# Splitting the output products of a decode attention kernel into two column groups with their own PSUM banks, casts and stores

## Chip, core and metric

The kernel runs on one core of one Trainium2 chip. Times are device microseconds (us) of whole executions. The granted clock is the share of the full TensorE clock that the profile shows. A packet is one piece of a load, moved by one of the core's 16 DMA engines.

## The reference

It is one decode step: attention over a cache of 4,096 positions for 2 rows and 32 heads, mixed by a gate with a small MLP.

```python
g = sigmoid((x * gate_w).sum(-1, keepdims=True))
q = (x @ wq)                                   # 2 rows, 32 heads of 128
p = softmax(q . k_cache * 128 ** -0.5)         # k_cache, v_cache: 2 x 32 x 4096 x 128, bf16
a = (p . v_cache) @ wo                         # wo: 4096 x 512
b = relu(x @ w1) @ w2
out = g * a + (1 - g) * b                      # 2 x 512
```

The keys and values are 134 MB of the 145.46 MB that must be read.

## The kernel before

There are eight stages `s`, each of 8 heads of one row: 8.4 MB of keys and 8.4 MB of values. In a stage VectorE multiplies four parts of the keys by the query (`mult`). Three of the four parts are then summed in groups by TensorE through products with the identity (`red`), and finished by a short VectorE sum (`scores`). The second part is summed by VectorE alone, in 8.7 us.

```python
    for s in range(NS):
        ...                                  # work of stages s-1 and s-2 woven in
        mult(s, 2)
        scores(s, 1)                         # VectorE's own long sum
        red(s, 2)
        mult(s, 3)
        scores(s, 2)
        red(s, 3)
        if s == NS - 1:
            pv(s - 1)
        scores(s, 3)                         # waits for red(s, 3) on TensorE
        probs(s)
        ...
        if s + 2 < NS:
            load_k(s + 2)                    # two key buffers: waits until stage s is read
            load_v(s + 1)                    # one value buffer: waits for pv(s)
        if s == NS - 2:
            load_v(NS - 1)
            load_wo()                        # into the value buffer: waits for pv(NS - 2)
```

The tail accumulates 11 MLP products (issued early) and 32 attention products, each 512 columns wide with 2 rows of output, into one PSUM tile, then casts and stores it:

```python
    a_ps = apool.tile([B, D], fp32, name="a_ps")
    def accumulate(lhsT, rhs, start, stop):
        nc.tensor.matmul(a_ps, lhsT=lhsT, rhs=rhs, start=start, stop=stop)
    ...
    evac(s)
    wo_mm(0)                                 # 8 products with the first 1 MB of wo
    comb(s)                                  # the last selector product: lhsT is a selection matrix
    unpack(s)
    for g in range(1, NG):
        wo_mm(g)
    nc.vector.tensor_copy(out=res[:, : D // 2], in_=a_ps[:, : D // 2])
    nc.scalar.copy(out=res[:, D // 2 :], in_=a_ps[:, D // 2 :])
    nc.sync.dma_start(out=out[:, 0, :], in_=res)
```

wo comes in six loads: three of 1 MB, and the last 1 MB cut in pieces of 512, 256 and 256 KB.

The softmax here doesn't subtract the row's maximum and nothing guards it: scores larger than these inputs give would overflow.

## Time and profile before

| | us |
|---|---|
| median of 6 runs before the prediction | 347.06 (346.87 to 349.65) |
| span of the profiled run | 345.3 |
| wo loads issued from | 326.83 |
| last 16 output products | 338.81 to 342.42 |
| casts, store issued | 342.46, 342.90, 343.29 |

These lines are from the page of the kernel before: the DMA busy share in tenths in 40 equal slices of the span; the DMA queues with packets, MB and the share of the 16 engines' time; and the shares of the chain that ended last (the page's walk back from the last instruction, at each step to what released it).

```profile
DMA  7999999898999989899999999999999999989993
...
q1 hardware_dynamic: 4036, 145.46, 97.9%
q8 instruction: 8, 0.13, 0.2%
...
DVE 65%; PE 16%; DMA 12%; issue 5%; SPq 0%; ACT 0%; DVEq 0%
```

The chain names VectorE for 65%.

The timeline of the tail (start, duration, engine, line, operation, operands; in brackets the idle time before it and what ended it):

```profile
326.83 3.85 SPq L369 DMA_DIRECT2D vt<-in_A_wo_dram  x6
...
338.81 3.61 PE L354 MATMUL a_ps<-vt,OT_sb 128*2 128x512 bf16 x16 [0.61 <-DMA vt<-in_A_wo_dram]
...
342.46 0.41 DVE L439 CAST res<-a_ps 2x256 bf16<-2x256 f32 x1 [5.62 <-PE a_ps L354]
342.90 0.36 ACT L440 CAST res<-a_ps 2x256 bf16<-2x256 f32 x1 [18.35 <-DVE res L439]
343.29 0.33 SPq L441 DMA_DIRECT2D out_dram<-res  x1
```

The products run at 226 ns each, and ScalarE's cast starts only after VectorE's.

The waits of VectorE, with the total, how often, and the longest:

```profile
DVE sc L231 <- PE red L219: 38.4, 9, 5.2
DVE kt L210 <- DMA kt<-in_A_k_cache_dram: 22.7, 1, 22.7
```

38.4 us are spent waiting for the identity matmuls (`red`). The 22.7 us are the start, when the first keys have not landed.

### The profile page before, as it was taken

Reading aid. Unit: us, or ns where it says so; the run is one execution under the profiler, and the core shown is the slowest. Engines: PE = TensorE matmul, PEld = TensorE weight load, DVE = VectorE, ACT = ScalarE, POOL = GpSimd, SP = SyncE. Lnnn points to the kernel's source line nnn. Section 1 sums busy time; section 2 is a strip of 40 time slices with the busy share of each in tenths; the row PEclk is TensorE's granted clock in tenths of the full one; section 3 lists DMA queues with packets and bytes.
Section 4 is the critical chain, followed back from the end, with each engine's and each line's share of the span. In section 5 each row is a group of like instructions: output and inputs, shape, how many; then the busy total and the mean of one; then the engine's idle time right before and its main releaser. Section 6 shows DMA issues by size and latency. Waiting matters only on the chain.

```text
span 345.3 us, 2525 instructions
## 1 busy us (share of the span) xinstructions
PE 182.3 (53%) x1107; PEld 76.0 (22%) x1107; DVE 254.1 (74%) x151; ACT 7.5 (2%) x23; POOL 6.1 (2%) x16
## 2 busy tenths in 40 slices
PE   0420685158506843655644761566165464477965
PEld 0100232023202311222211320223022221132432
DVE  3002269949994999499967999499939996799530
ACT  1010000000000000000000000000000000000000
POOL 7000000000000000000000000000000000000000
PEclk9995566788978888689868887889768896688999
DMA  7999999898999989899999999999999999989993
GB/s 308 474 433 392 464 440 478 372 486 364 480 395 455 478 375 471 387 463 397 448 478 395 463 397 448 410 440 473 402 455 410 440 419 425 478 387 418 416 410 141
DMA packets 4051, 145.60 MB, mean 422 GB/s; under 512 B 453, under 2 KB 586, under 8 KB 970
## 3 DMA queue, kind: packets, MB, share of 16 engines
q1 hardware_dynamic: 4036, 145.46, 97.9%
q8 instruction: 8, 0.13, 0.2%
q14 instruction: 1, 0.01, 0.0%
q10 hardware_dynamic: 6, 0.00, 0.0%
HBM read 145.46 MB, written 0.00 MB: 421 GB/s over the span
## 4 chain that ended last, share of the span: by engine, by line
DVE 65%; PE 16%; DMA 12%; issue 5%; SPq 0%; ACT 0%; DVEq 0%
DVE kt L210 37%; DVE sc L231 20%; PE red L219 14%; DMA kt<-in_A_k_cache_dram 9%; DVE PT_sb L251 4%; DMA vt<-in_A_wo_dram 3%; DVE osb L289 2%; PE a_ps L354 1%; PE o_ps L276 1%; DVE OT_sb L316 1%; DVE tmp L307 0%; DVE osb L287 0%; DVE rsg L268 0%; SPq L369 0%; DVE rsg L267 0%
## 5 line engine op out<-in xcount | busy, mean ns | idle before, releaser
L219 PE MATMUL red<-kt,ident 128*128 128x512 bf16 x400 | 125.5, 484 | 123.1 <-DVE kt L210 123.1
L210 DVE TENSOR_TENSOR kt<-kt,qb 128x8192 bf16<-128x8192 bf16 x32 | 141.3, 4417 | 31.5 <-DMA kt<-in_A_k_cache_dram 22.7
L219 PEld LDWEIGHTS <-ident 128*128 128x128 bf16 x400 | 47.9, 120 | 199.1 <-issue 163.5
L231 DVE TENSOR_REDUCE sc<-kt 128x64 f32<-128x8192 bf16 x7 | 60.8, 8679 | 0.0
L231 DVE TENSOR_REDUCE sc<-red 128x64 f32<-128x512 f32 x25 | 17.2, 687 | 38.4 <-PE red L219 38.4
L276 PE MATMUL o_ps<-vt,PT_sb 128*32 128x512 bf16 x448 | 27.1, 398 | 10.2 <-DMA vt<-in_A_v_cache_dram 10.2
L276 PEld LDWEIGHTS <-PT_sb 128*32 128x32 bf16 x512 | 14.7, 100 | 25.1 <-issue 13.9
L251 DVE TENSOR_TENSOR PT_sb<-e,tmask 128x2048 bf16<-128x2048 bf16 x8 | 18.3, 2283 | 0.6 <-ACT e L237 0.6
L237 ACT ACTIVATE e<-sc 128x256 bf16<-128x256 f32 x8 | 3.3, 417 | 274.7 <-DVE sc L231 274.7
L289 DVE SCALAR_TENSOR_TENSOR osb<-o_ps,jmask,osb 128x128 f32<-128x128 f32 x24 | 8.4, 351 | 0.8
L354 PE MATMUL a_ps<-vt,OT_sb 128*2 128x512 bf16 x32 | 7.4, 378 | 2.2 <-DMA vt<-in_A_wo_dram 2.2
L257 PE MATMUL gs<-partials,heads 128*128 128x1 f32 x16 | 3.0, 259 | 9.7 <-ACT e L237 9.7
L195 PE MATMUL mm<-vt 128*32 128x512 bf16 x64 | 5.5, 505 | 4.9 <-DMA vt<-in_A_wq_dram 4.2
L307 DVE SCALAR_TENSOR_TENSOR tmp<-comb,rsg,umask 128x128 f32<-128x128 f32 x8 | 2.8, 347 | 4.1 <-PE comb L301 4.1
L257 PEld LDWEIGHTS gs<-partials,heads 128*128 128x128 f32 x16 | 2.4, 188 | 13.6 <-ACT e L237 11.3
L354 PE MATMUL a_ps<-vt,hT 128*2 128x512 bf16 x11 | 4.9, 630 | 0.5 <-ACT hT L347 0.5
L159 PE MATMUL comb<-ident,vt 2*128 2x2 bf16 (+1 forms) x8 | 0.6, 173 | 7.6 <-DMA vt<-in_gate_w_dram 5.4
L439 DVE CAST res<-a_ps 2x256 bf16<-2x256 f32 x1 | 0.4, 413 | 5.6 <-PE a_ps L354 5.6
L276 PE MATMUL o_ps<-kt,PT_sb 128*32 128x512 bf16 x64 | 3.8, 380 | 1.1 <-DMA kt<-in_A_v_cache_dram 1.1
L354 PEld LDWEIGHTS <-OT_sb 128*2 128x2 bf16 x32 | 2.7, 83 | 6.6 <-issue 2.8
L195 PEld LDWEIGHTS <-vt 128*32 128x32 bf16 x64 | 2.2, 119 | 7.8 <-issue 7.2
L287 DVE TENSOR_SCALAR osb<-o_ps,jmask 128x128 f32<-128x128 f32 x8 | 2.8, 347 | 1.2 <-PE o_ps L276 1.2
(40 smaller groups left out, 33.9 us busy)
## 6 DMA issues: line engine op xcount, KB each, us to landing
vt<-in_A_wq_dram SPq DMA_DIRECT2D x1, 4096.0 KB, 12.4
kt<-in_A_v_cache_dram SPq DMA_DIRECT2D x1, 4096.0 KB, 25.9
kt<-in_A_v_cache_dram SPq DMA_DIRECT2D x2, 2048.0 KB, 34.8
vt<-in_A_wo_dram SPq DMA_DIRECT2D x3, 1024.0 KB, 9.1
vt<-in_B_w_dram SPq DMA_DIRECT2D x1, 1376.0 KB, 34.2
vt<-in_B_w_dram SPq DMA_DIRECT2D x1, 1280.0 KB, 36.8
vt<-in_A_wo_dram SPq DMA_DIRECT2D x1, 512.0 KB, 10.9
vt<-in_A_wo_dram SPq DMA_DIRECT2D x2, 256.0 KB, 11.0
```

The source lines that it names most:

```text
L195: nc.tensor.matmul(ps[j * CG : (j + 1) * CG, :], lhsT=xbp[:, b, c, e, :], rhs=wq_v[:, c, 2 * j + e, :, :], start=(c == 0 and e == 0), stop ...
L210: nc.vector.tensor_tensor(out=kt, in0=kt, in1=q, op=ALU.mult)
L219: nc.tensor.matmul(ps, lhsT=ident, rhs=prod[:, :, j * RW : (j + 1) * RW], start=(j == 0), stop=(j == Dh // RW - 1),)
L231: nc.vector.reduce_sum(out=sc_t[s][:, u * CU : (u + 1) * CU], in_=red_t.pop((s, u)), axis=AX.X)
L237: nc.scalar.activation(out=e, in_=sc_t.pop(s), func=ACT.Exp, scale=inv_sqrt_dh, accum_out=partials[:, s : s + 1],)
L251: nc.vector.tensor_tensor(out=out_, in0=e.to_broadcast(shape), in1=m.to_broadcast(shape), op=ALU.mult)
L257: nc.tensor.matmul(rs_t[s], lhsT=heads.rearrange("p t a -> p (t a)"), rhs=partials[:, s : s + 1], start=True, stop=True,)
L276: nc.tensor.matmul(o_t[s][k * CG : (k + 1) * CG, :], lhsT=PT_sb[:, s % 2, q, :], rhs=v_t[s][:, q * JB : (q + 1) * JB, :], start=(q < NCG), ...
L287: nc.vector.tensor_scalar_mul(osb, o[:, 0, :], jmask[:, 0:1])
L289: nc.vector.scalar_tensor_tensor(out=osb, in0=o[:, j, :], scalar=jmask[:, j : j + 1], in1=osb, op0=ALU.mult, op1=ALU.add,)
L316: nc.vector.reduce_sum(out=OT_sb[:, g, :, b], in_=tmp, axis=AX.X)
L354: nc.tensor.matmul(a_ps, lhsT=lhsT, rhs=rhs, start=start, stop=stop)
```

## The change

The intent is to let the products of two halves of the columns run side by side in two column groups of the TensorE array, to give each half its own bank so that the two casts need not take turns, and to store each half as soon as it is cast. The bank of the small sums is given up for it. The last selector product goes ahead of all output products.

```diff
-    a_ps = apool.tile([B, D], fp32, name="a_ps")
+    halves = []
+    for e in range(2):
+        a_ps = apool.tile([P, D // 2], fp32, name=f"a_ps{e}")
+        halves.append((e * CG, a_ps[e * CG : e * CG + B], slice(e * (D // 2), (e + 1) * (D // 2))))
 ...
-        rs_t[s] = gsp.tile([P, 1], fp32, name="gs")
+        rs_t[s] = mmp.tile([P, NG * Dh], fp32, name="mm")[:, :1]
 ...
-        nc.tensor.matmul(a_ps, lhsT=lhsT, rhs=rhs, start=start, stop=stop)
+        for _, a, cols in halves:
+            nc.tensor.matmul(a, lhsT=lhsT, rhs=rhs[:, cols], start=start, stop=stop)
 ...
-    wo_mm(0)
     comb(s)
     unpack(s)
-    for g in range(1, NG):
+    for g in range(NG):
         wo_mm(g)
-    res = ...  # two casts in turn, one store
+    copies = (nc.vector.tensor_copy, nc.scalar.copy)
+    for (p, a, cols), copy, queue in zip(halves, copies, (nc.sync, nc.scalar)):
+        res = consts.tile([P, D // 2], bf16, name=f"res{p}")[p : p + B]
+        copy(out=res, in_=a)
+        queue.dma_start(out=out[:, 0, cols], in_=res)
```

Each of 43 products becomes two, and each product is two instructions (weights, matmul). The program therefore has 86 more TensorE rows.

More of the change, by code (lines that the diff above doesn't have):

```diff
@@ L71 @@
     combp = ctx.enter_context(tc.tile_pool(name="combp", bufs=1, space=PS))
-    gsp = ctx.enter_context(tc.tile_pool(name="gsp", bufs=1, space=PS))
     apool = ctx.enter_context(tc.tile_pool(name="apool", bufs=1, space=PS))
@@ L431 @@
     evac(s)
-    wo_mm(0)
     comb(s)
     unpack(s)
-    for g in range(1, NG):
+    for g in range(NG):
         wo_mm(g)
-    res = consts.tile([B, D], bf16, name="res")
-    nc.vector.tensor_copy(out=res[:, : D // 2], in_=a_ps[:, : D // 2])
-    nc.scalar.copy(out=res[:, D // 2 :], in_=a_ps[:, D // 2 :])
-    nc.sync.dma_start(out=out[:, 0, :], in_=res)
+    copies = (nc.vector.tensor_copy, nc.scalar.copy)
[3 more added lines that the diff above has]
+        queue.dma_start(out=out[:, 0, cols], in_=res)
 _INS = ['A_x', 'A_k_cache', 'A_v_cache', 'A_wq', 'A_wo', 'B_x', 'B_w1', 'B_w2', 'gate_w']
```

## The prediction

> **What bounds the kernel now.** The span is 345.3 us. In the chain of work that ended last, VectorE has 65%, TensorE 16%, DMA 12%: from 32.7 us to 323 us it is VectorE's products and sums (L210, L231) and the identity matmuls they wait for (5.0 to 5.8 us of wait in stages 1 to 6). None of that is touched. The change works on the last 22 us, and on 11 matmuls at 45.9 us.
>
> In order of time, the tail of the chain reads: the wo loads until 338.76; 16 output products from 338.81 to 342.42 (3.61 us, 226 ns each at granted clock 1.00); VectorE cast 342.46, 0.41 us; ScalarE cast 342.90, 0.36 us, which waited for VectorE's; store issued 343.29; then about 2 us for its landing and the program's end.
>
> **What the change does.**
> 1. Each 512-column product becomes two of 256 columns in different column groups and banks. The trace already shows column groups overlapping: the last 64 o_ps matmuls (512 columns, four groups) take 3.64 us, 57 ns each, against 226 ns for a lone a_ps product. Two groups should give about 113 ns for a pair, so 16 products need about 1.8 us instead of 3.6. The Trainium skill ("TensorE: Matmul & The Clock Gate", Part 3) says the same of column tiles.
> 2. But the weights bind then. In the windows by stage, DMA share is still 0.65 from 339.0 to 340.0 and reaches zero only near 340.8; products of the last rows wait for their own pieces. I expect the last piece at about 340.9, two pairs after it (0.23 us) and the pipeline's end: casts start near 341.35 instead of 342.46. So about 1.1 us of the 1.8 us is kept.
> 3. The casts run side by side. Now one waits for the other; the Trainium skill ("PSUM — Partial Sum Buffer", bank collisions) says that two engines may not read one bank in the same quadrant at once, which is why they were ordered. Separate banks take 0.4 us off. Both stores land side by side; I allow 0.1 us for the second.
> 4. The last selector product ahead of the output products: it frees nothing that counts. Now it runs at 335.64, OT_sb is ready at 336.8, and the product that needs it waits for weights until 338.8. Worth 0.
> 5. The 11 MLP products at 45.9 us take 4.86 us at clock 0.50; perhaps 2.4 us after. TensorE is then idle until 55.26 anyway, and the V load behind them issues 2 us earlier onto a busy DMA queue. Worth 0.
> 6. Sharing the mm bank with the small sums: no other user is alive by then. Worth 0.
>
> **Prediction.** Sum: 1.1 + 0.4 = 1.5 us off 347.06: 345.6 us, 0.4% faster; range 344.9 to 346.7. Chances: faster by over 2% 0.01, within 2% 0.98, slower by over 2% 0.01.
>
> **What would show it.** Right: in the timeline the output products come in bursts of about 0.9 us for 8 pairs, with waits for wo before the last ones; both casts start within 0.1 us; the store issues near 341.7; VectorE's chain before 323 us keeps its times. Wrong: pairs at 226 ns (no overlap), no wait for the last wo pieces, casts still in turn, or the ScalarE store landing last by far.
>
> **What would make it wrong.** A later DMA tail (the slowest engine's last packets), a lower TensorE clock from the gaps between bursts, or a shift of the clock's phase in the stages, which moves 5 us waits by some tenths.

## More of the kernel before

The queue line says that the 16 DMA engines were at work for 97.9% of the span, and the slice line reads 8 or 9 tenths everywhere but in the first and the last slice. Note also the line `q8 instruction`: the program's own instructions come by DMA too, 8 packets, 0.13 MB, so 16 KB each.

## The result

The changed kernel took 347.9 us in the median of 10 runs (347.10 to 349.11). The kernel before took 347.45 in the median of 20 runs (346.76 to 349.90). The ratio of the means is 0.9999, with an interval of 0.9975 to 1.0023. The predicted 1.5 us did not come, and the time lies outside the predicted range.

The same parts of the page of the changed kernel:

```profile
DMA  8999999898999989999999999999999999999994
...
q1 hardware_dynamic: 4036, 145.46, 98.0%
q8 instruction: 9, 0.15, 0.2%
...
DVE 65%; PE 16%; DMA 12%; issue 5%; SPq 1%; DVEq 0%
```

These lines look nearly alike. The one difference that turns out to count: `q8 instruction` has 9 packets now, not 8. The timeline of the changed kernel's tail:

```profile
328.31 3.31 SPq L372 DMA_DIRECT2D vt<-in_A_wo_dram  x6
...
338.49 0.27 PE L357 MATMUL a_ps_140<-vt,OT_sb 128*2 128x256 bf16 x1 [1.45 <-DMA vt<-in_A_wo_dram]
...
341.89 0.37 PE L357 MATMUL a_ps_140<-vt,OT_sb 128*2 128x256 bf16 x1 [1.03 <-DMA vt<-in_A_wo_dram]
...
342.53 0.37 PE L357 MATMUL a_ps_140<-vt,OT_sb 128*2 128x256 bf16 x1
...
343.15 0.41 DVE L443 CAST res_1564<-a_ps_140 2x256 bf16<-2x256 f32 x1 [7.58 <-PE a_ps_141 L357]
343.18 0.36 ACT L443 CAST res_1567<-a_ps_141 2x256 bf16<-2x256 f32 x1 [17.15 <-PE a_ps_141 L357]
343.57 0.26 ACTq L444 DMA_DIRECT2D out_dram<-res_1567  x1
343.59 0.33 SPq L444 DMA_DIRECT2D out_dram<-res_1564  x1
```

Three things can be read. The overlap works: in the same view the pairs after 338.49 follow each other in 0.11 us, half of the 226 ns before. The casts start 0.03 us apart, so they no longer take turns. But the last two bursts of products wait for wo until 341.89 and 342.53 (the chain that ended last has the wo load until 342.48), while the old kernel's last product was finished at 342.42. The time was won and then waited away.

Where did the last pieces of wo come so late? I read the packet records of the trace (start and length of each packet; the engine is not recorded, but back-to-back chains show it). In the kernel before, the last wo packet ended at 340.85 us. After, all but one chain were done by 340.92, and one chain went on alone:

```
start us   ns    bytes      (changed kernel, the records from 341.0 us until the store)
341.001   227    2048
341.214    38       4      <- completion of the 5th load on this engine
341.224   206    2048
341.427    85    2048
341.508    84    2048
341.588    84    2048
341.668    84    2048
341.748    84    2048
341.828    84    2048
341.908    84    2048
341.988     9       4      <- completion of the 6th and last load
```

Shortly before, the ninth 16 KB instruction packet had started at 339.70 us and taken 0.88 us. The Trainium skill ("DMA: Bandwidth & Descriptors", section "Queues, rings and completion order") says that each engine takes packets by turns from the queues that have work for it. This trace agrees in so far as the fetch stands alone between two wo packets of the lone chain: it ended at 340.59, and the next wo packet started there. That packet and the three after it took 206 to 232 ns each, where the other chains' 2,048-byte packets took 84: 0.56 us more, after the fetch was over. Why is not shown. The same follows fetches elsewhere: after the seventh, at 282.81, the next 64 KB packet of the chain took 2.89 us instead of 2.42. So a fetch cost its engine some 1.4 to 1.6 us here, and not only its own 0.9 to 1.1.

A second difference lies in the body. The wo loads were issued at 328.31 instead of 326.83, because waits for identity matmuls were longer (40.9 us in sum, against 38.4). One of these, in stage 1 (columns: the stretch; busy time and count for PE, PEld, DVE, ACT, POOL; granted clock, DMA share, GB/s), first before, then after:

```profile
97.00:109.00 12.00, 5.00 (x16) 1.80 (x15) 7.50 (x4) 0.00 (x0) 0.00 (x0) 0.72 1.01 437
```
```profile
97.00:109.00 12.00, 6.48 (x16) 2.12 (x15) 6.03 (x4) 0.00 (x0) 0.00 (x0) 0.57 1.01 437
```

16 identity matmuls took 5.00 us at a mean granted clock of 0.72, and 6.48 us at 0.57. The Trainium skill ("TensorE: Matmul & The Clock Gate", Part 1) describes a full and a half clock, switched by recent activity in windows of 3.4 us that do not start with the kernel. The trace agrees: its clock records hold 1.00 and 0.50 only, nearly all in multiples of 3.413 us, at other times in the two runs.

So there were three theories. **D**: the DMA stream bounds both kernels, and the 86 additional instructions cost a ninth instruction fetch, which delays one DMA engine at the end by about what the change saves. **V**: VectorE's chain bounds, as predicted. **P**: the gain is there, and the clock's phase hid it in this sample.

### The profile page after: what moved, and what is told of

It reads as the page before. It is cut to its first block, busy times and chain, and to the rows that moved or that the text cites. A ratio compares the mean times of both kernels' runs of the same rounds, so it can differ in the third digit from the quotient of the medians. Undisturbed runs are those within 1.5% of the kernel's fastest.

```text
span 345.7 us, 2613 instructions
## 1 busy us (share of the span) xinstructions
PE 181.0 (52%) x1150; PEld 76.5 (22%) x1150; DVE 254.1 (73%) x151; ACT 7.5 (2%) x23; POOL 6.1 (2%) x16
## 4 chain that ended last, share of the span: by engine, by line
DVE 65%; PE 16%; DMA 12%; issue 5%; SPq 1%; DVEq 0%
DVE kt L212 37%; DVE sc L233 20%; PE red L221 14%; DMA kt<-in_A_k_cache_dram 9%; DVE PT_sb L253 4%; DMA vt<-in_A_wo_dram 3%; DVE osb L291 2%; PE o_ps L278 1%; SPq L372 1%; DVE OT_sb L318 1%; DVE tmp L309 0%; DVE osb L289 0%; DVE rsg L270 0%; DVE rsg L269 0%; PE a_ps_140 L357 0%
## 5 line engine op out<-in xcount | busy, mean ns | idle before, releaser
L221 PE MATMUL red<-kt,ident 128*128 128x512 bf16 x400 | 132.2, 504 | 130.1 <-DVE kt L212 130.1
L221 PEld LDWEIGHTS <-ident 128*128 128x128 bf16 x400 | 49.6, 124 | 210.5 <-issue 178.3
L233 DVE TENSOR_REDUCE sc<-red 128x64 f32<-128x512 f32 x25 | 17.2, 686 | 40.9 <-PE red L221 40.9
L278 PE MATMUL o_ps<-vt,PT_sb 128*32 128x512 bf16 x448 | 25.5, 380 | 3.9 <-DVE tmp L309 2.5
L278 PEld LDWEIGHTS <-PT_sb 128*32 128x32 bf16 x512 | 13.7, 97 | 16.8 <-issue 4.6
L259 PE MATMUL mm<-partials,heads 128*128 128x1 f32 x16 | 3.0, 259 | 9.7 <-ACT e L239 8.3
L357 PE MATMUL a_ps_140<-vt,OT_sb 128*2 128x256 bf16 x32 | 5.2, 299 | 3.1 <-DMA vt<-in_A_wo_dram 3.1
L259 PEld LDWEIGHTS mm<-partials,heads 128*128 128x128 f32 x16 | 2.4, 188 | 13.5 <-ACT e L239 11.3
L357 PE MATMUL a_ps_141<-vt,OT_sb 128*2 128x256 bf16 x32 | 5.2, 299 | 0.0
L303 PE MATMUL comb<-osb,pick 128*128 128x128 f32 x16 | 3.3, 285 | 1.7 <-DVE osb L291 1.7
```

What stands on the lines that cost most here:

```text
L221: nc.tensor.matmul(ps, lhsT=ident, rhs=prod[:, :, j * RW : (j + 1) * RW], start=(j == 0), stop=(j == Dh // RW - 1),)
L233: nc.vector.reduce_sum(out=sc_t[s][:, u * CU : (u + 1) * CU], in_=red_t.pop((s, u)), axis=AX.X)
L259: nc.tensor.matmul(rs_t[s], lhsT=heads.rearrange("p t a -> p (t a)"), rhs=partials[:, s : s + 1], start=True, stop=True,)
L278: nc.tensor.matmul(o_t[s][k * CG : (k + 1) * CG, :], lhsT=PT_sb[:, s % 2, q, :], rhs=v_t[s][:, q * JB : (q + 1) * JB, :], start=(q < NCG), ...
L357: nc.tensor.matmul(a, lhsT=lhsT, rhs=rhs[:, cols], start=start, stop=stop)
```

## Experiments

All had 5 rounds, each beside the kernel before on the same chip. Experiments 1, 2 and 4 ran together on one chip, the others on a second; the kernel before had medians of 347.63 us on the first and of 347.10 and 347.20 on the second. Where a time of experiments 3 and 5 to 10 is set against one of experiments 1, 2 and 4, the ratios are the fairer measure. Names: the "reordered" kernels carry this edit, which keeps all work and moves VectorE's long sum behind the fourth product:

```diff
+        if s < NS - 1:
             mult(s, 2)
-            scores(s, 1)
             red(s, 2)
             mult(s, 3)
+            red(s, 3)
+            scores(s, 1)
             scores(s, 2)
-            red(s, 3)
+        else: ...          # the last stage as before
```

### 1. The changed kernel again

No edit.

> The changed kernel once more, unedited, for a second trace and ten more times. Theory D (the DMA stream bounds both kernels; one extra 16 KB instruction fetch, on the ninth place, shares one DMA engine with the last wo pieces and makes it last): a ninth instruction fetch between 338 and 341 us again, one engine's last packet about 1 us after the other fifteen, time within 0.5 us of 347.8. Theory P (the first sample of ten was unlucky in the phase of TensorE's clock): the fetch is no fixed thing, and the mean falls to about 347.0, 1 us under the kernel before of the same rounds.

Measured: 347.68 us (347.14 to 348.08, 6 runs), ratio 0.9999 again. The ninth fetch came at 339.53, the last wo packet ended at 342.06; the chain before it was done at 340.60. The products waited for it:

```profile
341.87 1.03 PE L357 MATMUL a_ps<-vt,OT_sb 128*2 128x256 bf16 x8 [0.58 <-DMA vt<-in_A_wo_dram]
```

So the late engine is no accident of one run, and theory P's expected gain did not come.

### 2. The kernel before, reordered

> The kernel before, with the fourth product and its two sums put ahead of VectorE's own long sum in stages 0 to 6, so that VectorE no longer waits 5 to 6.5 us in each stage for the identity matmuls. Theory V (VectorE's chain bounds, as the prediction read it): seven waits of 5.5 us gone, time falls by 30 us or more, to about 315 us. Theory D: DMA engines were busy 99.8% already, so the time stays within 1.5 us of 346.9, the floor of the kernel before's own runs, and its spread shrinks to some tenths, since no run starves the wo loads any more.

Measured: 347.31 us (346.98 to 347.93), ratio 0.9990 (0.9967 to 1.0013). VectorE's waits in this kernel:

```profile
DVE kt L210 <- DMA kt<-in_A_k_cache_dram: 50.9, 6, 22.3
...
DVE sc L231 <- PE red L219: 6.4, 5, 3.1
```

The wait for identity matmuls fell from 38.4 to 6.4 us, and the wait for keys rose from 22.7 us in one place to 50.9 in six. 32 us of waiting moved to the DMA and nothing was won. wo was issued at 322.63, 4.2 us earlier than in the kernel before, and its last packet still ended at 340.63 (340.85 before). Theory V falls: the chain that the prediction followed is not what bounds. The DMA share from 2 to 330 us reads 1.00 (the last number but one) in both, the kernel before first:

```profile
2.00:330.00 328.00, 173.21 (x1057) 72.54 (x1057) 250.79 (x140) 6.77 (x22) 4.76 (x9) 0.81 1.00 431
```
```profile
2.00:330.00 328.00, 166.44 (x1057) 72.45 (x1058) 251.99 (x144) 6.75 (x22) 4.78 (x9) 0.76 1.00 431
```

What the edit does do is narrow the spread, though less than to the some tenths expected: 0.95 us here, over 6 runs, where the kernel before spread over 2.6 us in 11 runs of the same rounds. That the wide spread is the clock's phase, through late wo loads, fits the traces (after: DMA share 0.94 and 311 GB/s from 328 to 330 us, where the value loads ran out before wo was issued) but was not tested by itself.

### 3. The reordered kernel before, with less to load

```diff
-        load(t, kv_view(A_v_cache, s), ... [0, NC])
+        load(t, kv_view(A_v_cache, s), ... [0, 3 * NC // 4] if s == 3 else [0, NC])
+        if s == 3:
+            nc.gpsimd.memset(t[:, 3 * NC // 4 :, :], 0.0)
```

> The reordered kernel before with a quarter of one value tile (2.1 MB) not loaded but zeroed on GpSimd (wrong on purpose). At the 432.7 GB/s of the 64 KB packets that is 4.85 us of the DMA stream. DMA-bound: 342.5 us, plus or minus 0.5. Bound by the engines' chain: unchanged at 347.3.

Measured: 342.56 us (341.90 to 342.92), ratio 0.9852, 4.75 us under the reordered kernel's median (1.38% by the two ratios, 4.8 us). The bytes left out, at the rate of the 64 KB packets, are 4.85 us. The bytes set the time.

### 4. The changed kernel, reordered, with and without the ninth fetch

The first is the reordering alone; the second leaves 42 of 64 query products out (a wrong result, which the comparison with the reference still passed), to bring TensorE's rows from 2,254 to 2,170.

```diff
-        for c in range(DC):
+        some = range(1) if b == 0 else range(DC)
+        for c in some:
             for e in range(2):
-                for j in range(NCG):
+                for j in range(NCG if b == 0 or c == 0 else 1):
 ...                                 # stop= follows
```

> The changed kernel with the same move of VectorE's sums. Theory D: within 1 us of the reordered kernel before; the extra instruction fetch still delays one DMA engine by about 1 us near the end and takes back most of what the overlapped products and casts save (about 0.8 us). Theory P: 1 us faster than the reordered kernel before, because the body no longer depends on the clock's phase and the tail's gain shows.

> The reordered changed kernel with 42 of the 64 query products left out (a wrong result on purpose), so that TensorE runs about as many instructions as in the kernel before (2170 rows against 2168; 2254 with the change). Theory D: eight instruction fetches instead of nine, no lone engine at the end, and 0.7 to 1.1 us less than the reordered changed kernel. Theory P, or any theory in which the fetch is harmless: no difference.

Measured: 347.15 us (347.04 to 347.23) with nine fetches, and 345.86 us (345.74 to 346.04) with eight. The first, in the queue lines of its page and in its timeline:

```profile
q8 instruction: 9, 0.15, 0.2%
```
```profile
338.67 1.04 PE L357 MATMUL a_ps<-vt,OT_sb 128*2 128x256 bf16 x16 [0.20 <-DMA vt<-in_A_wo_dram]
...
341.94 0.85 PE L357 MATMUL a_ps<-vt,OT_sb 128*2 128x256 bf16 x8 [1.41 <-DMA vt<-in_A_wo_dram]
...
342.82 0.41 DVE L451 CAST res<-a_ps 2x256 bf16<-2x256 f32 x1 [6.57 <-PE a_ps L357]
...
343.25 0.26 ACTq L452 DMA_DIRECT2D out_dram<-res  x1
343.26 0.32 SPq L452 DMA_DIRECT2D out_dram<-res  x1
```

and the second, in the same two views:

```profile
q8 instruction: 8, 0.13, 0.2%
```
```profile
335.38 6.08 PE L358 MATMUL a_ps<-vt,OT_sb 128*2 128x256 bf16 x64
...
341.50 0.41 DVE L452 CAST res<-a_ps 2x256 bf16<-2x256 f32 x1 [5.33 <-PE a_ps L358]
...
341.92 0.26 ACTq L453 DMA_DIRECT2D out_dram<-res  x1
341.94 0.32 SPq L453 DMA_DIRECT2D out_dram<-res  x1
```

With nine, the last 8 matmuls wait 1.41 us for wo, and the last packet ended at 341.91. With eight, it ended at 340.59 and the casts start 1.32 us earlier. That is the whole difference of 1.29 us in time, and theory D's reading of the fetch holds. With eight, the products run almost without a pause, most of them at a granted clock of 0.50; by the single records only the last two pairs start 0.1 us late, at 341.08, 0.49 us after the last packet. There TensorE and the last packet end nearly together. Theory P falls with the same pair: with the runs this close together, the reordered changed kernel is only 0.16 us under the reordered kernel before, not 1. The tail of the reordered kernel before:

```profile
337.29 5.34 PE L354 MATMUL a_ps<-vt,OT_sb 128*2 128x512 bf16 x24
...
342.66 0.41 DVE L447 CAST res<-a_ps 2x256 bf16<-2x256 f32 x1 [4.59 <-PE a_ps L354]
...
343.50 0.32 SPq L449 DMA_DIRECT2D out_dram<-res  x1
```

Against it (347.31), the change without its ninth fetch is worth 1.45 us: 1.16 us to the casts, 0.40 us more to the store.

### 5. The same on the unreordered kernel

The 42 query products left out of the changed kernel as it stands.

> The changed kernel as it stands (VectorE's order as before), with 42 query products left out (wrong on purpose), 2170 rows. Fetch theory: 1.0 to 1.4 us under the changed kernel's 347.8, so a mean near 346.6 and lowest runs near 345.8, with the same spread of 1 to 3 us as the kernel before, because the body still starves the wo loads in some runs. Rival: the loss of the changed kernel lies in its body (TensorE colder after stage 0) and it stays near 347.8.

Measured: 346.60 us (345.73 to 347.76), ratio 0.9966 (0.9941 to 0.9992). Its profile has eight fetches, but fell on a late body: wo was issued at 328.16, several engines ended only at 342.0, and the casts came at 343.51. So it is 1.1 to 1.3 us under the two medians of the changed kernel, within a spread of 2 us; the intervals of the ratios (up to 0.9992 here, from 0.9974 there) still touch.

### 6. A ninth fetch without the split

The reordered kernel before, with one query product issued 43 times more, early, and overwritten.

```diff
+        for i in range(43 if b == 0 else 0):
+            nc.tensor.matmul(
+                ps[:CG, :], lhsT=xbp[:, b, 0, 0, :], rhs=wq_v[:, 0, 0, :, :], start=True, stop=True
+            )
```

> The reordered kernel before, unsplit, with 43 more query products issued early and overwritten (a right result), 2254 rows as in the changed kernel. Fetch theory: a ninth 16 KB fetch appears near 339.5 us though nothing was split; one engine's last packet moves to about 341.9; the products of the last rows wait for it, so the time rises by 0.3 to 0.7 us over the reordered kernel before (347.3): less than 1.1, as TensorE was late there by itself. If the split and not the number of instructions made the late engine: no ninth fetch and no change.

Measured: 347.76 us (347.58 to 348.36), 0.45 us over the reordered kernel before. By the ratios (1.0011 against 0.9990) it is 0.7 us, and their intervals overlap, so the cost in time is not clear of noise. The trace is clear:

```profile
q8 instruction: 9, 0.15, 0.2%
```
```profile
341.06 1.89 PE L358 MATMUL a_ps<-vt,OT_sb 128*2 128x512 bf16 x8 [0.63 <-DMA vt<-in_A_wo_dram]
```

The ninth instruction packet came at 338.09, and the last wo packet ended at 341.86. So the number of instructions makes the late engine, not the split. That the cost is smaller because unsplit products were late by themselves fits the tail in experiment 4, where they run until 342.63 without a wait.

The traces also show when a fetch falls due: the eight of the kernel before come about 265 recorded TensorE instructions apart, the last after 2,052 of 2,230, so a ninth would have come after the end. In the changed kernel it came after 2,281 of 2,316.

### 7. The ninth fetch earlier

The same 43 additional products in the reordered changed kernel.

> The reordered changed kernel with 43 query products more, early and overwritten (right result), 2340 rows: the ninth fetch comes 86 instructions earlier, near 335 us, in the middle of the wo loads. If a fetch costs its DMA engine the same anywhere in the saturated stream, 347.1 us as without them; if only a fetch among the last small pieces hurts, down to 345.9 us.

Measured: 347.08 us (346.91 to 347.31), the same as without them. The ninth fetch came at 330.20 and the last packet still ended at 341.73. The last four products again waited for wo, until 342.27. Moving the fetch to the start of the wo loads did not help. One position was tried, so nothing is said of a fetch far earlier.

### 8. Both halves in one column group

The reordered changed kernel without the ninth fetch, so casts, banks and stores apart, but no overlap of products:

```diff
-        halves.append((e * CG, a_ps[e * CG : e * CG + B], ...))
+        halves.append((0, a_ps[:B], ...))
```

> The reordered changed kernel without the ninth fetch (42 query products left out, wrong on purpose), with both halves in the same column group, so products cannot overlap but banks, casts and stores stay apart. Tells the two gains apart: if the parallel casts are worth 0.4 us and the overlap the rest, the time is 346.9, between the reordered kernel before (347.3) and the run without fetch (345.9); if the overlap is worth nothing, because the weights bind, it stays at 345.9.

Measured: 348.77 us (348.08 to 349.36), a miss: 1.46 us slower than the reordered kernel before (0.47% by the ratios, 1.6 us), where 0.4 us faster was expected.

The tail in its timeline, and two stretches of the tail with the granted clock as third number from the end:

```profile
336.02 8.62 PE L358 MATMUL a_ps<-vt,OT_sb 128*2 128x256 bf16 x64
...
344.57 0.41 DVE L452 CAST res<-a_ps 2x256 bf16<-2x256 f32 x1 [7.76 <-PE a_ps L358]
```
```profile
335.40:337.00 1.60, 1.60 (x7) 0.98 (x8) 0.64 (x2) 0.00 (x0) 0.00 (x0) 0.50 1.00 412
337.00:339.00 2.00, 2.00 (x12) 1.18 (x10) 0.00 (x0) 0.00 (x0) 0.00 (x0) 0.50 0.94 371
```

Its 64 products start only at 336.0, behind the selector product, and run without a pause until 344.6, for the first 3 us at half clock. My sum had left out both. The overlap is therefore needed to afford the late start, and the two gains can't be read apart from this run.

### 9. The selector product alone

The reordered kernel before, with `wo_mm(0)` put behind `comb(s)` and `unpack(s)`.

> The reordered kernel before with only the last selector product moved ahead of the output products. Output products then start near 336.6 instead of 333.5 us (they wait behind the selector product), and 32 of them at 226 ns need 7.2 us: end near 343.8 instead of 342.6, so 1.1 us slower than the reordered kernel before (348.4 us). The prediction's reading (worth 0) gives 347.3.

Measured: 349.31 us (348.38 to 349.53), 2.0 us slower than the reordered kernel before (0.53% by the ratios, 1.8 us); 1.1 was expected.

The output products in its timeline, and the same two stretches:

```profile
335.29 9.28 PE L354 MATMUL a_ps<-vt,OT_sb 128*2 128x512 bf16 x32
```
```profile
335.40:337.00 1.60, 1.60 (x5) 0.42 (x4) 0.64 (x2) 0.00 (x0) 0.00 (x0) 0.50 1.03 425
337.00:339.00 2.00, 2.00 (x6) 0.59 (x5) 0.00 (x0) 0.00 (x0) 0.00 (x0) 0.50 0.95 374
```

The 32 products stand behind the selector product until 335.3 and take 9.28 us, 290 ns each instead of 226, since the clock is at 0.50 until past 339. So "worth 0" fails here. What it is worth beside overlapped products was not tested. In the reordered kernels TensorE sits longer in the tail waiting for values, so the size of this loss need not hold for the unreordered one.

### 10. A correct version without the ninth fetch

The reordered changed kernel, with more of the sums taken by VectorE in its new slack, which removes 48 identity matmuls with their weight loads: 2,158 rows. First tried in stages 0 to 2, then in 2, 3 and 5.

```diff
-        if u in DVE_SUMS and s < NS - 1:
+        if (u in DVE_SUMS and s < NS - 1) or (u == 2 and s < 3):              # first
+        if (u in DVE_SUMS and s < NS - 1) or (u == 2 and s in (2, 3, 5)):     # mended
```

> A correct version meant to beat both: the reordered changed kernel, with the third part of the sums of stages 0 to 2 taken by VectorE too, so that 48 identity matmuls fall away and TensorE runs 2158 instruction rows. If the ninth fetch was what the reordered changed kernel lost, the result is within 0.4 us of the run with query products left out (345.9 us), about 1.4 us under the reordered kernel before. If the wrong query values or the missing early matmuls were the cause there, it stays at 347.1.

Measured: 349.22 us (348.41 to 350.23), a miss. The fetches were eight, but stages 0 to 2 ended late, their key buffers came free late, and the DMA engines ran dry: idle for 0.56 us between 70 and 80 us, the following 64 KB packets were slower (2,513 ns in the mean from 60 to 80 us, 2,418 is the median of this run), and the last wo packet ended at 343.58. The last values came late too: the output products started only at 338.44 and ran without a wait for wo until 344.5.

> The correct version mended: VectorE takes the third sums of stages 2, 3 and 5 instead of 0 to 2, where the trace of the reordered kernel shows VectorE waiting 5 us and more for its keys, so no load is released late. 2158 instruction rows, no ninth fetch. Expected 345.7 to 346.2 us, 0.5% under the kernel before and 1.4 us under the reordered kernel before. If the longer VectorE stages starve the DMA queue again, idle DMA time shows inside the body and it stays over 347.

Measured: 345.80 us (345.75 to 346.12), ratio 0.9948 (0.9924 to 0.9973). Its instruction queue, and its casts and a store in the timeline:

```profile
q8 instruction: 8, 0.13, 0.2%
```
```profile
341.08 0.38 PE L357 MATMUL a_ps<-vt,OT_sb 128*2 128x256 bf16 x4 [0.16 <-DMA vt<-in_A_wo_dram]
...
341.50 0.41 DVE L451 CAST res<-a_ps 2x256 bf16<-2x256 f32 x1 [5.31 <-PE a_ps L357]
...
341.94 0.32 SPq L452 DMA_DIRECT2D out_dram<-res  x1
```

This is a right result, faster than both kernels, and it shows the same cast and store times as the run with query products left out. So the gain there was not owed to the wrong queries. Beside experiment 7, which ran in the same rounds on the same chip with nine fetches, it is 1.28 us faster: the 1.29 us of experiment 4 once more.

### Side by side

The last wo packet is read from the packet records of one profiled run each, the time is the median.

| kernel | fetches | last wo packet | casts from | time |
|---|---|---|---|---|
| before | 8 | 340.85 | 342.46 | 347.1 to 347.6 |
| changed | 9 | 341.99 | 343.15 | 347.7 to 347.9 |
| before, reordered | 8 | 340.63 | 342.66 | 347.31 |
| the same with 43 products more | 9 | 341.86 | 342.98 | 347.76 |
| changed, reordered | 9 | 341.91 | 342.82 | 347.15 |
| the same with 43 products more | 9 | 341.73 | 342.68 | 347.08 |
| the same with 42 products less | 8 | 340.59 | 341.50 | 345.86 |
| the same with 48 identity matmuls less (stages 2, 3, 5) | 8 | 340.62 | 341.50 | 345.80 |

## Why the prediction was wrong

- **"What bounds the kernel now": wrong.** It named VectorE's products, sums and their waits. The DMA stream bounds. Taking 32 us of those waits away changed nothing (experiment 2), and taking 2.1 MB away gave 4.75 us (experiment 3). The share of DMA time, 97.9%, stood on the page.
- **Step 1, pairs at 113 ns: right.** Measured 109 ns at clock 1.00. In the last bursts of the changed kernel the clock had fallen to 0.50 and pairs took 0.17 to 0.21 us, as the list of risks allowed.
- **Step 2, "I expect the last piece at about 340.9": the step that failed.** The last packet ended at 341.99 and 342.06 in two profiles of the changed kernel. The prediction did not count the 86 additional instructions at all. They are also bytes: a ninth 16 KB fetch on one of the saturated DMA engines, worth 1.29 us between experiments with and without it. The list of risks did name a later DMA tail, "the slowest engine's last packets", but without a cause or a size. The casts came at 343.15, 1.80 us after the predicted 341.35. Of this the late packet is 1.09 us (341.99 for 340.9). Another 0.54 us passed from the last packet to the product (342.53), where the estimate let the products follow at once, and 0.17 us are slower products behind it. Where the fetch was absent, in the reordered kernel, the casts came at 341.50 against the predicted 341.35, and that is partly luck: the last packet came 0.3 us earlier than expected (340.59), which made up for most of the 0.5 us from packet to product that was left out.
- **Step 3, the casts side by side: right.** They start 0.03 us apart. From the first cast to the store's issue it took 0.83 us before and 0.44 after, which saves 0.39 for the predicted 0.4. The Trainium skill ("PSUM — Partial Sum Buffer", on bank collisions) explains why one bank had made them take turns; the trace agrees with both orders.
- **Step 4, the selector product worth 0: not shown.** No run has the overlapped products without this move. Alone, in the reordered kernel, it cost 2.0 us.
- **Step 5, the MLP products worth 0: right.** They took about 1.3 us instead of 4.9, since the clock was at 1.00 there in this run, and the value load behind them was issued at 46.28 instead of 50.80. The last packet of the last value load still ended at 330.55, against 330.85, since the DMA queue was full.
- **Step 6, the shared bank worth 0:** not tested by itself. VectorE's chain shows no new wait for it.
- **The sum and the range.** The overlap and the parallel casts are real, and the predicted 1.5 us came as 1.45 us in the reordered pair once the fetch was gone; that the two sizes agree so well is partly luck, as under step 2. The term that the sum lacked is the fetch, about 1.3 us. The range also ignored that the kernel before spreads over 3 us from run to run.

What stays open: why the packets that follow a fetch on its engine take about 0.5 us more in sum; why one engine was 0.4 us behind the others at the end of experiment 8, with eight fetches (341.22); and how the loss of the changed kernel divides, in the mean of its unreordered runs, between the fetch (about 1 us by experiment 5) and late bodies.

## What to carry to other kernels

When the DMA engines are busy from end to end, look at the time of the last byte and at what follows it; a chain through a compute engine may have slack that only an experiment shows. Instructions are DMA traffic too: before doubling a group of small instructions, count the rows, compare the instruction packets on the page, and see whether another fetch falls into a saturated stream (here one came about every 265 recorded TensorE instructions). If it does, pay for it elsewhere, by taking as many instructions out as you put in.

## What the Trainium skill lacked or had wrong

- "Runtime: NRT & Kernel Launch", "Instruction fetch mechanics": it gives refills of 16 KiB, 256 instructions each, and calls the cost of crossing such a boundary mostly hidden. The size agrees: 16,384 bytes each (rows of 64 bytes, by "Perfetto Trace Analysis", make 256 to a fetch), 8 for 2,168 TensorE rows and 9 for 2,254, on the queue that the profile calls q8. The cost does not: a fetch takes one DMA engine some 0.9 to 1.1 us (once 1.8), the packets after it take about 0.5 us more, and one more fetch on a saturated stream made the last packet 1.1 to 1.3 us later and the kernel 1.29 us slower. "DMA: Bandwidth & Descriptors" names the refill only as traffic of row 14 and gives no cost.
- "DMA: Bandwidth & Descriptors", "Specifications": it gives about 358 GB/s as the limit of HBM for one core, and only a later section, "Bandwidth", says that this is the share when both cores of an HBM domain stream. This core read 421 GB/s over the whole span, and 432.7 GB/s at the rate of its 64 KB packets. The page's fabric ceiling of 435 GB/s fits.
- No page that I read gives the time from the last packet of a load on the sync queue to the matmul that waits for it (the breakdown of a load's fixed cost in "DMA: Bandwidth & Descriptors" is for loads issued by GpSimd): here 0.54 us (341.99 to 342.53).
- "TensorEngine Tiling (Array Packing)", "Performance Considerations", lists what tiling gains and what it costs in PSUM evacuation, but not that the split doubles the instruction count: here 86 rows more, which cost 1.29 us through the fetch.
